# The last group's first six pairs with w_out as seven half products in 128x32 column tiles, its partial sums kept in SBUF for the last two pairs

## The chip, the cores and the metric

One core of one Trainium2 chip. The time is the device time of one execution in microseconds (us); the kernel before took 267.31 us in the median of three runs (266.57 to 267.91). The comparison is between the kernel before and the kernel with the change, both on one core.

## The reference, cut to what matters

A polynomial-sketch attention makes a matrix `x` of 4352 tokens by 128 features (4 heads of 32). That matrix goes through a two-layer block with an ELU between, and this block is where the change is:

```
h = x @ w_in                      # 4352x128 @ 128x2048
g = np.where(h > 0.0, h, np.exp(np.minimum(h, 0.0)) - 1.0)
out = (g @ w_out).astype(np.float32)   # 4352x2048 @ 2048x128
```

All of it is in 32-bit floats.

## The kernel before, in words

The 4352 tokens are cut into NQ = 9 groups: groups 0 to 7 have 512 tokens, the last, group 8, has 256 (`qn[8]` is 2, times 128). The 2048 hidden features are NP = 8 pairs `cp` of two blocks of 128. A *step* is one (group, pair). The list `steps` (lines 901 and 902) fixes their order; groups 2 to 8 go one after another, each through its eight pairs. The order of instructions on every engine is the order of the Python text (`manual_schedule`), and waits between engines are put in by the framework where a tile is read or written.

The main loop (lines 995 to 1033) does this in turn number n:

- `mm1(g, cp)`, line 768: TensorE makes `h`, two banks (c = 0, 1) of 128 features by the group's tokens. It goes through `quarters` (line 223), which splits one product in four matmuls with 32 columns of the stationary operand each, on the four 128x32 column tiles of the array. `h` has four banks, so two steps are in flight.
- `elu`, line 800: ScalarE makes relu(-h) and then exp of its negative (lines 789, 791); VectorE makes `gg` = max(e - 1, h) (line 797). `gg` has three buffers.
- For groups 2 to 7 (`seven(g)`) `sums7` (line 700) makes four sums of quarters of `gg` on GpSimd.
- The product with w_out for the step of two turns ago. For groups 0 and 1 it is `mm2`. For groups 2 to 7 it is `mm2_seven` (line 713), Strassen's scheme in Winograd's form: seven products of half size in place of eight, accumulated over the pairs in seven columns of two PSUM banks `pa` and `pb`. The sums of w_out that it needs are in `SS`, made once by `weights7` (line 692). At a group's end `fin_seven_copy`, `fin_seven_a` and `fin_seven_b` (lines 733 to 766) put the seven sums together on ScalarE and VectorE, transpose them in 32x32 blocks and send them out in 16 DMAs, all issued by SyncE (SP), line 765.
- For group 8 it is `mm2_last` (line 826): `gg` is the stationary operand, w_out the moving one (128 columns), so the output has tokens on partitions and needs no transpose. Per pair it has four products (two blocks c, two token halves i), each four column tiles: 16 matmuls of 128 columns. They accumulate in two PSUM tiles `ol`. `fin_last` (line 836) copies one tile with ScalarE and the other with VectorE and sends each in two DMAs, one issued by SP and one by ScalarE.

A 32-bit matmul stands in the trace as two records, and so does its weight load (LDWEIGHTS, row PEld).

Of the kernel before, what the change touches and what calls it, by code (L numbers as in the profile page):

```python
# [12 lines left out]
F32 = mybir.dt.float32  # L13
ALU = mybir.AluOpType
U32 = mybir.dt.uint32
MUL, ADD, SUB, MAX = ALU.mult, ALU.add, ALU.subtract, ALU.max
# [6 lines left out]
def _ap(ap: bass.AP, free):  # L23
    return dataclasses.replace(ap, ap=[list(ap.ap[0])] + [list(x) for x in free])
# [3 lines left out]
def kernel(  # L28
# [21 lines left out]
    nc = tc.nc  # L50
    B, H, S, D = q.shape
    R = S1.shape[0]
    P = 128
# [3 lines left out]
    NP = NC // 2  # L57
# [7 lines left out]
    work = ctx.enter_context(tc.tile_pool(name="wk", bufs=2))  # L65
    psum = ctx.enter_context(tc.tile_pool(name="psum", bufs=2, space=bass.MemoryType.PSUM))
# [82 lines left out]
    W = const.tile([P, NP, 4 * P], F32, name="W")  # L149
# [73 lines left out]
    def quarters(dst, lhs, rhs, **kw):  # L223
        for c in range(4):
            nc.tensor.matmul(dst[32 * c:32 * c + 32], lhs[:, 32 * c:32 * c + 32], rhs, skip_group_check=True,  # L225
                             tile_position=(0, 32 * c), **kw)
# [226 lines left out]
    NQ = (NH + 7) // 8  # L453
# [6 lines left out]
    def half_tile(g, k):  # L460
        return divmod(8 * g + k, NT)
# [218 lines left out]
    hs, es, gs, ops = {}, {}, {}, {}  # L680
# [5 lines left out]
    def seven(g):  # L686
        return 2 <= g < NQ - 1

    SS = const.tile([P, 4, NP, 64], F32, name="SS")
    ts, acc, sas = {}, {}, {}  # L690
# [6 lines left out]
    def quarter(g, cp, c, y):  # L697
        return gs[g, cp][:, c].rearrange("p (u x s) -> p u x s", u=2, x=2)[:, :, y, :]

    def sums7(g, cp, c):  # L700
        if c == 0:
            ts[g, cp] = work.tile([P, 4, 2, P], F32, name="tt", tag="raw", bufs=6)
        t = ts[g, cp]
        b11, b12 = (quarter(g, cp, 0, y) for y in range(2))
        if c == 0:
            nc.gpsimd.tensor_tensor(t[:, 0], b12, b11, op=SUB)  # L706
            return
        b21, b22 = (quarter(g, cp, 1, y) for y in range(2))
        nc.gpsimd.tensor_tensor(t[:, 2], b22, b12, op=SUB)  # L709
        nc.gpsimd.tensor_tensor(t[:, 1], t[:, 2], b11, op=ADD)  # L710
        nc.gpsimd.tensor_tensor(t[:, 3], b21, t[:, 1], op=SUB)  # L711

    def mm2_seven(g, cp, first, last):
        if first:
            acc[g] = [psum.tile([P, 512], F32, name="pa", tag="o0", bufs=1),
                      psum.tile([P, 512], F32, name="pb", tag="o1", bufs=1)]
        a, b = acc[g]
        t, w = ts.pop((g, cp)), [W[:, cp, 2 * P + 64 * i:2 * P + 64 * i + 64] for i in range(4)]
        b11, b21, b22 = quarter(g, cp, 0, 0), quarter(g, cp, 1, 0), quarter(g, cp, 1, 1)
        p1, p2, p6 = (a, 0, w[0], b11), (a, 1, w[2], b21), (a, 2, SS[:, 1, cp], t[:, 1])  # L720
        p4, p5 = (b, 0, w[3], t[:, 3]), (b, 1, SS[:, 0, cp], t[:, 0])
        p7, p3 = (b, 2, SS[:, 2, cp], t[:, 2]), (b, 3, SS[:, 3, cp], b22)
        todo = [p1, p2, p6, p3, p5, p7, p4] if first or last else [p1, p2, p3, p5, p7, p6, p4]
        for i, (bank, col, lhs, rhs) in enumerate(todo):
            for u in range(2):
                for w in range(2):
                    r = 64 * u + 32 * w
                    nc.tensor.matmul(bank[r:r + 32, P * col:P * col + P], lhs[:, 32 * w:32 * w + 32], rhs[:, u],  # L728
                                     start=(first and i in (0, 3)), stop=last, skip_group_check=True,
                                     tile_position=(0, r))  # L730
        del gs[g, cp]
# [14 lines left out]
    def fin_seven_b(g):  # L746
        b = acc.pop(g)[1]
        uu, cc = sas.pop(g)
        pb = b[:].rearrange("p (k s) -> p k s", s=P)
        nc.vector.tensor_tensor(uu[:, 1:], _ap(uu[:, 0], [[0, 2], [1, P]]), pb[:, 1:3], op=ADD)  # L750
        nc.vector.tensor_tensor(cc[:, 2:], _ap(uu[:, 2], [[0, 2], [1, P]]), pb[:, 0:2], op=ADD)
        nc.vector.tensor_tensor(cc[:, 1], uu[:, 1], pb[:, 3], op=ADD)
        ob = work.tile([P, 2, 4, 2, D], F32, name="ob7", tag="ob", bufs=2)
        nc.vector.transpose(ob[:].rearrange("p h k w d -> p (h k w d)"), cc[:].rearrange("p k s -> p (k s)"))
        rows = out.rearrange("(b w y t) (e l d) -> b w e l y t d", b=B, w=2, t=NT, e=2, l=2)
        for u in range(2):
            k = 0
            while k < 4:
                bt, t = half_tile(g, 4 * u + k)
                m = min(4 - k, NT - t)  # L760
                for lo in range(2):
                    r = slice(64 * u + 32 * lo, 64 * u + 32 * lo + 32)
                    for hi in range(2):
                        for w in range(2):
                            nc.sync.dma_start(rows[bt, w, hi, lo, :, t:t + m, :], ob[r, hi, k:k + m, w, :])
                k += m

    def mm1(g, cp, cs=(0, 1)):
        n = qn[g] * P
        if 0 in cs and (g, cp) not in hs:  # L770
            hs[g, cp] = [psum.tile([P, 512], F32, name="h", tag="h", bufs=4) for c in range(2)]
        for c in cs:
            quarters(hs[g, cp][c][:, :n], W[:, cp, c * P:c * P + P], xg[g][:, :n])
# [8 lines left out]
    def elu_a(g, cp, c, parts=(0, 1)):  # L782

        n = qn[g] * P
        if c == 0 and 0 in parts:
            es[g, cp] = work.tile([P, 2, 512], F32, name="e", tag="e", bufs=2)
        e = es[g, cp][:, c, :n]
        if 0 in parts:
            nc.scalar.activation(e, hs[g, cp][c][:, :n], RELU, scale=-1.0)  # L789
        if 1 in parts:  # L790
            nc.scalar.activation(e, e, EXP, scale=-1.0)  # L791
# [8 lines left out]
    def elu(g, cp, c):  # L800
        elu_a(g, cp, c)
        elu_d(g, cp, c)
# [23 lines left out]
    def mm2_last(cp, first, last):  # L826
        g = NQ - 1
        if first:
            ops[g] = [psum.tile([P, P], F32, name="ol", tag=t, bufs=k) for t, k in (("o0", 1), ("aux", 2))]
        gg = gs.pop((g, cp))  # L830
        for a in range(4):
            c, i = (a % 2, a // 2) if last else divmod(a, 2)
            quarters(ops[g][i][:], gg[:, c, i * P:i * P + P], W[:, cp, (2 + c) * P:(3 + c) * P],
                   start=(first and c == 0), stop=(last and c == 1))

    def fin_last():
        g, n = NQ - 1, qn[NQ - 1]
        o = work.tile([P, 2, P], F32, name="ol", tag="ol", bufs=1)
        rows = out.rearrange("(b y t) f -> b y t f", b=B, t=NT)
        for i, copy in enumerate((nc.scalar.copy, nc.vector.tensor_copy)):  # L840
            copy(o[:, i, :], ops[g][i][:])
            for u, eng in enumerate((nc.sync, nc.scalar)):
                b, t = half_tile(g, u * n + i)
                eng.dma_start(rows[b, :, t, :], o[64 * u:64 * u + 64, i])
# [150 lines left out]
    for n in range(2, N + 2):  # L995
        if n < N:
            g, cp = steps[n]
            mm1(g, cp)
        for f, *a in extra.get(n, ()):
            f(*a)  # L1000
        if n < N:
            elu(g, cp, 0)
            if seven(g):
                sums7(g, cp, 0)
            for f, *a in extra.get((n, 0), ()):
                f(*a)
            before = steps[n - 2]
            ends = n > 3 and seven(before[0]) and before[1] == NP - 1
            if ends:
                elu_a(g, cp, 1, (0,))  # L1010
                mm2_seven(*before, False, True)
                fin_seven_copy(before[0])
                elu_a(g, cp, 1, (1,))
                fin_seven_a(before[0])
                elu_d(g, cp, 1)
            else:
                elu(g, cp, 1)
            if seven(g):
                sums7(g, cp, 1)
            if ends:  # L1020
                fin_seven_b(before[0])
        for f, *a in extra.get((n, 1), ()):
            f(*a)
        g, cp = steps[n - 2]
        if g == NQ - 1:
            mm2_last(cp, cp == 0, cp == NP - 1)
        elif seven(g):
            if cp < NP - 1:
                mm2_seven(g, cp, cp == 0, False)
        elif n > 2:  # L1030
            mm2(g, cp, cp == 0, cp == NP - 1)
            if cp == NP - 1:
                fin1(g)
    fin_last()


# [27 lines left out]
```

## Time and profile before

| what | value |
|---|---|
| median of three runs | 267.31 us |
| the profiled execution's own time | 267.85 us |
| its span in the trace | 266.1 us |
| TensorE busy | 259.1 us (97%) |
| VectorE, ScalarE, GpSimd busy | 187.8, 184.0, 160.6 us |
| granted TensorE clock | full speed in all slices after the first |
| group 8's `mm1`, 128x256 matmuls | 8.4 us busy, x128 records |
| group 8's `mm2_last`, 128x128 matmuls | 8.1 us busy, x256 records |
| output DMAs of one group of 512 (line 765) | 16 issues by SP, 16 KB each for group 7 |
| DMA queue q8, kind "instruction" | 42 packets, 0.69 MB |

"Busy" is the union of the records of an engine; matmuls are pipelined, so a busy TensorE need not be at its peak. "SPq" and "ACTq" are the sequencers of SyncE and ScalarE: their records are issues of DMAs and waits for semaphores. A timeline line gives start, length, engine, line, operation and how many records it merges.

### The profile page before, as it was taken

What the parts mean: (1) busy time and instruction counts of PE and PEld (TensorE: products, weight loads), DVE (VectorE), ACT (ScalarE), POOL (GpSimd) and SP (SyncE); (2) the same over time, 40 slices, a digit from 0 to 9 for tenths busy, and PEclk for the clock granted to TensorE, in tenths of its full rate; (3) what the DMA queues carried; (4) which work ended last, traced back from release to release, by engine and by line L of the source; (5) the groups of instructions that cost most, each with busy time, mean ns of one, the idle gap of its engine ahead of it and who ended that gap; (6) DMA issues with size and microseconds to landing.
All of it is one profiled execution on the core that took longest, in us unless ns stands there. A gap on an engine that the chain in (4) does not pass through costs nothing.

```text
span 266.1 us, 12146 instructions
## 1 busy us (share of the span) xinstructions
PE 259.1 (97%) x5345; PEld 151.6 (57%) x5345; DVE 187.8 (71%) x347; ACT 184.0 (69%) x355; POOL 160.6 (60%) x233
## 2 busy tenths in 40 slices
PE   8999999999999999999999999999999999999993
PEld 7742223343334665667666666665666666657872
DVE  7799999997969796996567676744356446664641
ACT  2479978677567656785587777776777777777781
POOL 4400008204316985798859799898689888998200
PEclk9999999999999999999999999999999999999999
DMA  5999960011002200001100110001001100110011
GB/s 184 320 352 242 288 171 8 2 25 62 2 2 43 42 4 2 2 8 19 27 3 2 28 20 2 2 15 25 11 2 21 25 4 5 18 17 11 7 25 37
DMA packets 26420, 13.89 MB, mean 52 GB/s; under 512 B 19200, under 2 KB 24576, under 8 KB 26368
## 3 DMA queue, kind: packets, MB, share of 16 engines
q1 hardware_dynamic: 25920, 12.79, 19.0%
q8 instruction: 42, 0.69, 1.1%
q10 hardware_dynamic: 448, 0.33, 0.4%
q14 instruction: 10, 0.08, 0.1%
HBM read 10.88 MB, written 2.23 MB: 49 GB/s over the span
## 4 chain that ended last, share of the span: by engine, by line
PE 92%; DVE 4%; POOL 1%; issue 1%; ACT 0%; DVEq 0%
PE h L225 43%; PE pb L728 16%; PE pa L728 12%; PE o L225 11%; PE ol L225 3%; PE kv L390 1%; PE idle L230 1%; PE h L644 1%; PE qps L644 1%; DVE qp L582 1%; POOL kp L286 1%; PE kfps L322 1%; PE qps L538 1%; PE kv L225 1%; PE abp L303 1%
## 5 line engine op out<-in xcount | busy, mean ns | idle before, releaser
L797 DVE SCALAR_TENSOR_TENSOR gg<-e,h 128x512 f32<-128x512 f32 (+1 forms) x144 | 92.2, 653 | 63.3 <-ACT e L791 60.5
L225 PE MATMUL h<-xg,W 128*32 128x512 f32 (+1 forms) x1168 | 130.4, 563 | 0.0
L789 ACT ACTIVATE e<-h 128x512 f32<-128x512 f32 (+1 forms) x144 | 81.4, 566 | 49.6 <-PE h L225 48.1
L791 ACT ACTIVATE e<-e 128x512 f32<-128x512 f32 (+1 forms) x144 | 87.6, 608 | 4.4
L225 PEld LDWEIGHTS h<-xg,W 128*32 128x32 f32 x1168 | 38.4, 110 | 49.0 <-issue 38.9
L706 POOL TENSOR_TENSOR tt<-gg 128x256 f32<-128x256 f32 x48 | 35.4, 737 | 16.0 <-DVE gg L797 15.6
L709 POOL TENSOR_TENSOR tt<-gg 128x256 f32<-128x256 f32 x48 | 35.6, 742 | 13.4 <-DVE gg L797 13.2
L711 POOL TENSOR_TENSOR tt<-gg,tt 128x256 f32<-128x256 f32 x48 | 36.7, 765 | 3.8
L710 POOL TENSOR_TENSOR tt<-tt,gg 128x256 f32<-128x256 f32 x48 | 35.4, 738 | 3.8
L728 PEld LDWEIGHTS pa<-gg,W 128*32 128x32 f32 x768 | 22.8, 110 | 23.4 <-issue 22.4
L225 PE MATMUL o<-gg,W 128*32 128x512 f32 x256 | 30.6, 594 | 0.4 <-DVE W L129 0.4
L728 PE MATMUL pa<-gg,W 128*32 128x128 f32 x768 | 30.4, 273 | 0.0
L728 PE MATMUL pb<-tt,SS 128*32 128x128 f32 x768 | 30.3, 273 | 0.0
L728 PEld LDWEIGHTS pb<-tt,SS 128*32 128x32 f32 x768 | 22.5, 110 | 0.0
L728 PE MATMUL pb<-tt,W 128*32 128x128 f32 x384 | 20.1, 273 | 0.0
L728 PE MATMUL pb<-gg,SS 128*32 128x128 f32 x384 | 19.8, 273 | 0.0
L728 PE MATMUL pa<-tt,SS 128*32 128x128 f32 x384 | 19.8, 273 | 0.0
L126 POOL TENSOR_TENSOR raw<-raw,tiny 128x512 f32<-128x512 f32 x1 | 1.0, 1046 | 29.9 <-DVE raw L121 29.9
L225 PEld LDWEIGHTS o<-gg,W 128*32 128x32 f32 x256 | 7.8, 109 | 16.6 <-issue 14.2
L728 PEld LDWEIGHTS pb<-tt,W 128*32 128x32 f32 x384 | 12.1, 110 | 0.2 <-issue 0.2
L728 PEld LDWEIGHTS pa<-tt,SS 128*32 128x32 f32 x384 | 12.0, 110 | 0.0
L728 PEld LDWEIGHTS pb<-gg,SS 128*32 128x32 f32 x384 | 11.9, 110 | 0.1
(150 smaller groups left out, 245.4 us busy)
## 6 DMA issues: line engine op xcount, KB each, us to landing
raw<-in_moe_w_in_dram SPq DMA_DIRECT2D x8, 256.0 KB, 6.4
raw<-in_moe_w_out_dram SPq DMA_DIRECT2D x8, 256.0 KB, 6.5
hd_k<-in_k_dram SPq DMA_DIRECT2D x3, 544.0 KB, 7.3
hd_q<-in_q_dram SPq DMA_DIRECT2D x3, 544.0 KB, 7.8
v<-in_v_dram SPq DMA_DIRECT2D x4, 288.0 KB, 6.8
out_dram<-ob SPq DMA_DIRECT2D x72, 16.0 KB, 1.5
v<-in_v_dram SPq DMA_DIRECT2D x4, 256.0 KB, 6.6
out_dram<-ob SPq DMA_DIRECT2D x16, 32.0 KB, 1.6
```

The lines of the kernel that those rows point to most:

```text
L225: nc.tensor.matmul(dst[32 * c:32 * c + 32], lhs[:, 32 * c:32 * c + 32], rhs, skip_group_check=True, tile_position=(0, 32 * c), **kw)
L230: nc.tensor.matmul(idle[:, :cols], some[:, :P], some[:, :cols], skip_group_check=True)
L286: eng.tensor_mul(dst, _ap(a_, list(a_.ap[1:]) + [[0, R]]), _ap(b_, [b_.ap[1], [0, R], b_.ap[2]]))
L644: nc.tensor.matmul(ps[w][s * r:s * r + s, 64 * k:64 * (k + m)], lhs, qpT[g, i][rows, o + 2 * k:o + 2 * (k + m), f, :], start=(f == 0 and j ...
L706: nc.gpsimd.tensor_tensor(t[:, 0], b12, b11, op=SUB)
L709: nc.gpsimd.tensor_tensor(t[:, 2], b22, b12, op=SUB)
L710: nc.gpsimd.tensor_tensor(t[:, 1], t[:, 2], b11, op=ADD)
L711: nc.gpsimd.tensor_tensor(t[:, 3], b21, t[:, 1], op=SUB)
L728: nc.tensor.matmul(bank[r:r + 32, P * col:P * col + P], lhs[:, 32 * w:32 * w + 32], rhs[:, u], start=(first and i in (0, 3)), stop=last, s ...
L789: nc.scalar.activation(e, hs[g, cp][c][:, :n], RELU, scale=-1.0)
L791: nc.scalar.activation(e, e, EXP, scale=-1.0)
L797: nc.vector.scalar_tensor_tensor(gs[g, cp][:, c, :n], es[g, cp][:, c, :n], -1.0, hs[g, cp][c][:, :n], op0=ADD, op1=MAX)
```

## The change

For group 8 the pairs 0 to 5 go through seven half products as well, pairs 6 and 7 stay as they were. `b11, b12` and `b21, b22` are the two token halves of blocks c = 0 and c = 1. The sums of `gg` are made by `sums7_last`: two by GpSimd, two by VectorE. The sums of w_out come from `SS`, which is there already. Each of the seven products is four column tiles with 64 columns moving: 28 matmuls per pair. They accumulate over the six pairs in seven columns of 64 of one bank `pl`. After pair 5, `fin_seven_last` puts these into `cl` (two token halves by 128 outputs) with one copy on ScalarE and five additions on VectorE. It is called in the last turn with an `mm1`, after that turn's ELU. Pairs 6 and 7 accumulate in `ol` in PSUM as before, and `fin_last` adds `cl` and `ol`, both halves on VectorE.

```
     def mm2_last(cp, first, last):
...
-            ops[g] = [psum.tile([P, P], F32, name="ol", tag=t, bufs=k) for t, k in (("o0", 1), ("aux", 2))]
+            ops[g] = [psum.tile([P, P], F32, name="ol", tag=t, bufs=k) for t, k in (("o0", 1), ("o1", 1))]
...
+    def sums7_last(cp, c):
+        g = NQ - 1
+        (b11, b12), (b21, b22) = [[gs[g, cp][:, x, P * y:P * y + P] for y in range(2)] for x in range(2)]
+        if c == 0:
+            ts[g, cp] = work.tile([P, 4, P], F32, name="tl", tag="raw", bufs=6)
+        t = ts[g, cp]
+        if c == 0:
+            nc.gpsimd.tensor_tensor(t[:, 0], b12, b11, op=SUB)
+        else:
+            nc.vector.tensor_tensor(t[:, 2], b22, b12, op=SUB)
+            nc.vector.tensor_tensor(t[:, 1], t[:, 2], b11, op=ADD)
+            nc.gpsimd.tensor_tensor(t[:, 3], b21, t[:, 1], op=SUB)
+
+    def mm2_seven_last(cp, first, last):
+        g = NQ - 1
+        if first:
+            acc[g] = psum.tile([P, 512], F32, name="pl", tag="aux")
+        gg, t, w = gs.pop((g, cp)), ts.pop((g, cp)), [W[:, cp, 2 * P + 64 * i:2 * P + 64 * i + 64] for i in range(4)]
+        b11, b21, b22 = gg[:, 0, :P], gg[:, 1, :P], gg[:, 1, P:2 * P]
+        todo = [(0, w[0], b11), (1, w[2], b21), (6, SS[:, 3, cp], b22), (4, SS[:, 0, cp], t[:, 0]),
+                (5, SS[:, 2, cp], t[:, 2]), (2, SS[:, 1, cp], t[:, 1]), (3, w[3], t[:, 3])]
+        for i, (col, rhs, lhs) in enumerate(todo):
+            quarters(acc[g][:, 64 * col:64 * col + 64], lhs, rhs, start=(first and i == 0), stop=last)
+
+    def fin_seven_last():
+        g = NQ - 1
+        pl = acc.pop(g)[:, :448].rearrange("p (k d) -> p k d", d=64)
+        sa = work.tile([P, 2, 64], F32, name="sl", tag="sl", bufs=1)
+        uu = work.tile([P, 3, 64], F32, name="ul", tag="ul", bufs=1)
+        cl = sas[g] = work.tile([P, 2, 2, 64], F32, name="cl", tag="cl", bufs=1)
+        nc.scalar.copy(sa[:], pl[:, 1:3])
+        nc.vector.tensor_tensor(uu[:, 0], sa[:, 1], pl[:, 0], op=ADD)
+        nc.vector.tensor_tensor(cl[:, 0, 0], sa[:, 0], pl[:, 0], op=ADD)
+        nc.vector.tensor_tensor(uu[:, 1:], _ap(uu[:, 0], [[0, 2], [1, 64]]), pl[:, 4:6], op=ADD)
+        nc.vector.tensor_tensor(cl[:, :, 1], _ap(uu[:, 2], [[0, 2], [1, 64]]), pl[:, 3:5], op=ADD)
+        nc.vector.tensor_tensor(cl[:, 1, 0], uu[:, 1], pl[:, 6], op=ADD)
+
     def fin_last():
...
-        for i, copy in enumerate((nc.scalar.copy, nc.vector.tensor_copy)):
-            copy(o[:, i, :], ops[g][i][:])
+        cl = sas.pop(g)
+        for i in range(2):
+            nc.vector.tensor_tensor(o[:, i, :], cl[:, i].rearrange("p h d -> p (h d)"), ops[g][i][:], op=ADD)
...
             elu(g, cp, 0)
             if seven(g):
                 sums7(g, cp, 0)
+            if g == NQ - 1 and cp < NP - 2:
+                sums7_last(cp, 0)
...
             if ends:
                 fin_seven_b(before[0])
+            if g == NQ - 1 and cp < NP - 2:
+                sums7_last(cp, 1)
...
-        if g == NQ - 1:
-            mm2_last(cp, cp == 0, cp == NP - 1)
+        if g == NQ - 1 and cp < NP - 2:
+            mm2_seven_last(cp, cp == 0, cp == NP - 3)
+            if cp == NP - 3:
+                fin_seven_last()
+        elif g == NQ - 1:
+            mm2_last(cp, cp == NP - 2, cp == NP - 1)
```

## The prediction

> **What bounds the kernel now.** I read the page's chain first, then the chain in order of time, then the end of the timeline. On the page TensorE holds nearly all of the chain:
>
> ```profile
> PE 259.1 (97%) x5345; PEld 151.6 (57%) x5345; DVE 187.8 (71%) x347; ACT 184.0 (69%) x355; POOL 160.6 (60%) x233
> ...
> PE 92%; DVE 4%; POOL 1%; issue 1%; ACT 0%; DVEq 0%
> ```
>
> In order of time its last lines (start, length) are:
>
> ```profile
> 256.26 0.86 PE h L225 x16
> 257.13 0.87 PE ol L225 x32
> 258.00 0.86 PE h L225 x16
> 258.86 2.66 PE ol L225 x96
> ```
>
> A step of the last group is 0.86 + 0.87 = 1.73 us, without a gap. But TensorE ends at 261.5 and the span at 266.1. What lies behind shows in the timeline of the other engines:
>
> ```profile
> 251.49 9.97 SPq L765 DMA_DIRECT2D out_dram<-ob  x16
> 261.56 2.36 SPq L844 DMA_DIRECT2D out_dram<-ol  x2
> ```
> ```profile
> 261.11 0.27 ACT L841 COPY ol<-ol 128x128 f32<-128x128 f32 x1 [1.06 <-PE ol L225]
> 261.41 1.77 ACTq L844 DMA_DIRECT2D out_dram<-ol  x2
> ```
> ```profile
> 261.55 0.29 DVE L841 COPY ol<-ol 128x128 f32<-128x128 f32 x1 [1.04 <-PE ol L225]
> ```
>
> The reader is to see that SP issues DMAs without a pause from 251.49 to 263.92. First come the 16 output DMAs of group 7, up to 261.46, then the two of group 8. The first result was there at 261.38 and the second at 261.84, but SP issued the second from 263.29 only, because the issue before it took long:
>
> ```profile
> L844 SPq DMA_DIRECT2D out_dram<-ol x2: 630/1131/1632, 261.6 to 263.3; - x2
> ```
>
> So the end hangs on SP's queue, and TensorE is about level with it. Issues of line 765 take 430 ns, a few far more. The DMA view says which. Two stretches, 255.2 to 258.3 and 258.15 to 261.5:
>
> ```profile
> q8 instruction: 1, 0.02, 2.1%
> out_dram<-ob SPq DMA_DIRECT2D x5, 16.0 KB, 2.7
> ```
> ```profile
> out_dram<-ob SPq DMA_DIRECT2D x7, 16.0 KB, 1.5
> ```
> ```profile
> L765 SPq DMA_DIRECT2D out_dram<-ob x7: 430/431/437, 258.2 to 261.0; - x7
> ```
>
> The second has no instruction packet and every issue is short; the first has one, at 256.73, and the issue begun at 256.59 took 1536 ns. The same holds at 251.93 (issue 1839 ns) and 261.56 (1632 ns). An issue in progress ends some 0.37 us after the packet (251.93 + 1.39, issue over at 253.69). In SP's last 12.4 us three such packets cost 1.41 + 1.11 + 1.00 = 3.52 us above 430 ns (630 for the last).
>
> **What the Trainium skill says.** "Runtime: NRT & Kernel Launch", section Instruction fetch mechanics: instructions come in 16 KiB blocks of 256, each sequencer's fetch driven by its own DMA queue, the cost mostly hidden. The size agrees: 42 packets of 0.69 MB together are 16.4 KB each, and TensorE's 2 x 5345 records are 41.8 blocks. "Mostly hidden" holds for TensorE, not for SP's issues. "TensorEngine Tiling (Array Packing)", section Performance Considerations: a matmul has some 60 cycles of overhead, so short moving operands gain nothing below that. 64 columns is near this edge; the trace has that shape (below) and it is still in proportion. "SBUF — State Buffer", section Who interferes with whom: a VectorE operation with two SBUF inputs contends with a GpSimd operation reading SBUF. The trace agrees: line 563 at 128x128 took 574 ns beside GpSimd, line 565 with one input in PSUM 288.
>
> **The change part by part.** Times from the profiled execution (span 266.06, own time 267.85; the median is 267.31).
>
> *TensorE.* Removed per pair: 32 records of 128 columns, 0.87 us, 27.2 ns each. Added: 56 of 64 columns. The same shape, 128x64 on 128x32 tiles with a new weight load each, ran here:
>
> ```profile
> 10.01 1.21 PE L390 MATMUL kv<-kp,v 128*32 128x64 f32 x72
> ```
>
> One record is 0.22 us long, so 71 starts took 0.99 us: 13.9 ns each. 56 x 13.9 = 0.78 us; gain 0.09 per pair, 0.55 over six. Bounds: 13.6 (half of 27.2; gain 0.65), and, if the 110 ns loads did not hide, 14 turns of the four tiles x 110 = 1.54 us, a loss of 4.0 over six.
>
> *Sums.* Per pair GpSimd gets two 128x128 operations, VectorE two. GpSimd is idle after 247.8; line 252, 128x128, took 402 ns. For VectorE the bounds are 293 (line 571 with GpSimd idle) and 574; I take 293, since GpSimd runs mostly at other times. VectorE then has about 0.35 + 0.42 + 2 x 0.32 = 1.4 us a step, under the new pitch of 0.86 + 0.78 = 1.64; ScalarE's four take about 1.45 from start to start. Behind VectorE's sums in its queue stands the next `gg`, for which the `h` banks wait; two steps of lead leave about 0.85 us. One place has no lead: pair 1, whose sums stand behind group 7's transpose (line 754, to 251.46). The two take until about 252.0, GpSimd's until 252.5, and the seventh product could otherwise start at 252.3 (250.00 + 0.78 + 0.86 + 0.66): a stall of about 0.35 us, 0 if that order is kinder. TensorE is left with about 0.2 us (0 to 0.65).
>
> At 574 ns VectorE needs 1.97 us a step, 0.33 too long; five steps make 1.65, less 0.85 of lead: results 0.8 us later.
>
> *Tail.* `fin_seven_last` stands behind the last ELU on ScalarE and VectorE, whose last `gg` starts 2.26 us after the last `mm1` starts (260.08 - 257.82). Then a copy (0.27) and five additions, in lines 743 to 752 0.2 apart when independent and 0.45 when dependent at double width; at 128x64 and 128x128 I reckon 0.15 and 0.32. The fifth starts about 3.4 after that `mm1`, line 881's two additions at 3.55 and 3.8, done at 4.1; before, the two copies were done at 3.56 and 4.02. With the `mm1` 0.1 earlier, the first result comes 0.3 us later than before (261.7), the second at 261.9, as before. The gain on TensorE ends here.
>
> *SP's queue.* No DMA is added, and group 7's 16 start at the same 251.49. But six pairs have 24 records more in matmuls and as many in loads: 6 x 48 = 288 instructions, 1.1 blocks. And the blocks come sooner: 112 + 32 = 144 instructions per 1.64 us, in place of 96 per 1.73. The packet of 251.93 came some 116 instructions after the first w_out products of the group began (250.00); now that is 250.8. It holds SP from 251.49 until 250.8 + 1.39 + 0.37 = 252.56 in place of 251.81: 0.75. The next come every 256 instructions, some 2.9 us: about 254, 257 and, slower since pairs 6 and 7 are as before, 260 to 261. SP is busy throughout, so each costs the mean of the three, 1.17: 3.52. In all 4.27 for 3.52 before: **+0.75 us**. If the packet comes only after 251.5, the first costs up to 1.41: +1.4. If the fourth does not come, -0.4. Both L884 issues on SP then start after 262.6, when their data (261.7, 261.9) lies ready.
>
> Sum: 266.06 + 0.75 = 266.8 of span, 268.6 for such an execution, and 267.31 + 0.75 = **268.0 us** for the median.
>
> **The rivals.**
> *A: the gain arrives.* If SP is ahead outside the profile, or the fourth packet falls away, the results set the end: between 0.5 us earlier (no stall, short tail) and level. For it: the chain names TensorE. Against: SP's record without a gap. About 267.0.
> *B: slower by over 0.5%* (1.34 us; about what a measurement of this kernel can tell from no change). One mechanism: every one of four packets hits an issue of SP in full. It decides from a mean of (3.52 + 1.34) / 4 = 1.21 us per packet; the three seen have 1.17, the largest 1.41. About 268.8. Against: the first should fall before 251.49.
> *C: the change doesn't do what it says*, 64-column products being no faster than the loads: +4.0, 271.3. Line 390 speaks against it.
> *D: VectorE's sums at 574 ns:* results at 262.7, still no later than SP's 262.6 to 263; about 268.1.
>
> **How the numbers follow.** Forecast 0.55 (267.4 to 268.5), A 0.25, B 0.13, C 0.02, D 0.05. The range leaves out C, part of B and A's far end, with three runs spread by 0.6 either way: 266.6 to 268.9. Faster by over 0.5% (under 265.97) would take all of A and more: 0.03. Slower by over 0.5% (over 268.65): B and C, with little else, 0.14. The rest, 0.83, is within.
>
> **What would show it.** Right: `pl` groups of 0.78 us; one gap in TensorE of some 0.3 us in the second; four instruction packets after 250.5, not three, and SP's last issue ending at about 264.6 in place of 263.92. Wrong: SP idle before L884's issues, or three packets only; then A. `pl` groups over 0.87: C. Line 847 and 848 over 0.5 us: D.

## The result, and the profile after

| | before | after |
|---|---|---|
| median, same chip, 11 runs each | 267.21 us (266.46 to 268.45) | 268.85 us (268.59 to 270.65) |
| ratio after/before, 95% interval | | 1.0072 (1.0053 to 1.0090) |
| profiled execution, its span | 267.85, 266.1 us | 269.15, 267.1 us |
| median span of many runs | 265.1 us (45 runs) | 266.7 us (11 runs) |

Slower by 0.7%, 1.6 us. The last row sets the profiles in place: the one execution of the kernel before that was profiled lies 1 us above that kernel's median span, that of the changed kernel 0.4 us above its own. Where the time went is in the timeline of TensorE. First the head of the page and the chain, of the changed kernel:

```profile
PE 259.2 (97%) x5489; PEld 150.5 (56%) x5489; DVE 192.8 (72%) x365; ACT 183.8 (69%) x355; POOL 165.6 (62%) x245
...
PE 89%; DVE 7%; ACT 2%; issue 1%; POOL 0%; DVEq 0%
```

144 matmul records and 144 load records more, as counted. The busy time of TensorE is all but the same, so the page shows no loss. The timeline of TensorE does (start, length, what, records, and in brackets the idle time before and the releaser that the trace infers). The first five lines are an undisturbed pair:

```profile
249.85 0.41 PE L225 MATMUL pl<-W,gg 128*32 128x64 f32 x16
250.07 0.29 PE L225 MATMUL pl<-SS,gg 128*32 128x64 f32 x8
250.19 0.52 PE L225 MATMUL pl<-SS,tl 128*32 128x64 f32 x24
250.52 0.29 PE L225 MATMUL pl<-W,tl 128*32 128x64 f32 x8
250.63 1.05 PE L225 MATMUL h<-xg,W 128*32 128x256 f32 x16
...
251.83 0.52 PE L225 MATMUL pl<-SS,tl 128*32 128x64 f32 x24
252.41 0.32 PE L225 MATMUL pl<-W,tl 128*32 128x64 f32 x8
...
253.75 0.52 PE L225 MATMUL pl<-SS,tl 128*32 128x64 f32 x24
254.37 0.32 PE L225 MATMUL pl<-W,tl 128*32 128x64 f32 x8
...
257.34 0.29 PE L225 MATMUL pl<-SS,tl 128*32 128x64 f32 x8
258.37 0.43 PE L225 MATMUL pl<-SS,tl 128*32 128x64 f32 x16 [0.73 <-DVE gg L797]
...
260.37 1.06 PE L225 MATMUL ol<-W,gg 128*32 128x128 f32 x32
262.37 1.08 PE L225 MATMUL ol<-W,gg 128*32 128x128 f32 x32 [0.94 <-DVE cl L873]
```

The pair's seven products start at 249.85 and the next `h` at 250.63: 0.78 us. So the products are as fast as the prediction said. But there are four gaps. Read them by starts, since a record's end is modelled: `pl` x24 is followed after 0.33 us in the first pair, after 0.58 in the second (252.41 - 251.83) and after 0.62 in the third; 8 records of `pl` take 0.11 us, but 257.34 to 258.37 is 1.03; 32 records of `ol` take 0.87, but 260.37 to 262.37 is 2.00. The gaps are 0.25, 0.29, 0.92 and 1.13 us, 2.59 together, against 0.55 gained. The kernel before has no such gap:

```profile
250.00 1.06 PE L225 MATMUL ol<-W,gg 128*32 128x128 f32 x32
...
258.68 2.80 PE L225 MATMUL ol<-W,gg 128*32 128x128 f32 x96
```

The 96 records are those of pairs 5, 6 and 7, so pair 7 starts at 258.68 + 2 x 0.87 = 260.42. From the group's first w_out product to that of pair 7 it is 12.52 us (249.85 to 262.37), and was 10.42: TensorE is 2.1 us later.

SP's queue in the changed kernel:

```profile
251.35 11.83 SPq L765 DMA_DIRECT2D out_dram<-ob  x16
263.40 1.19 SPq L884 DMA_DIRECT2D out_dram<-ol  x2
```

And VectorE's last additions:

```profile
263.08 0.72 DVE L881 TENSOR_TENSOR ol<-cl,ol 128x128 f32<-128x128 f32 x2 [0.75 <-PE ol L225]
```

SP is through with group 7 at 263.18, and the first result is there at 263.37: now the result comes last, and SP's first issue of line 884 follows it at once (263.40); the second, at 264.05, stands behind the first, 0.25 us after its data. Instruction packets came at 251.74, 255.51 and 259.43; the next only at 268.21, after the span.

### The profile page after: what moved, and what is told of

The parts are those of the page before. It is cut to its first block, busy times and chain, and to the rows that moved or that the text cites. A ratio compares the mean times of both kernels' runs of the same rounds, so it can differ in the third digit from the quotient of the medians.

```text
span 267.1 us, 12465 instructions
## 1 busy us (share of the span) xinstructions
PE 259.2 (97%) x5489; PEld 150.5 (56%) x5489; DVE 192.8 (72%) x365; ACT 183.8 (69%) x355; POOL 165.6 (62%) x245
## 4 chain that ended last, share of the span: by engine, by line
PE 89%; DVE 7%; ACT 2%; issue 1%; POOL 0%; DVEq 0%
PE h L225 41%; PE pb L728 15%; PE pa L728 12%; PE o L225 11%; PE kv L390 1%; PE idle L230 1%; PE h L644 1%; PE qps L644 1%; DVE gg L797 1%; PE abp L303 1%; ACT e L791 1%; DVE qp L582 1%; ACT e L789 1%; PE kfps L322 1%; PE qps L538 1%
## 5 line engine op out<-in xcount | busy, mean ns | idle before, releaser
L225 PEld LDWEIGHTS h<-xg,W 128*32 128x32 f32 x1168 | 37.4, 110 | 49.3 <-issue 40.1
L728 PE MATMUL pb<-tt,W 128*32 128x128 f32 x384 | 19.5, 273 | 0.0
```

## The experiments

**Three theories.** *F, supply of instructions:* TensorE runs dry. Count its instructions from the first `pl` product (every record of a matmul has one of a load, so x56 is 112). A pair with its `h` is 112 + 32 = 144. The third gap of the list above lies in pair 4 after 32 records: 4 x 144 + 64 = 640. The second lies in pair 2 after 48 records: 2 x 144 + 96 = 384. The fourth lies behind pair 5 (832, no `h` follows) and pair 6's 64: 896. They are 256 apart, one block as in the prediction. Each ends 1.35 to 1.49 us after an instruction packet is through (251.74 + 1.20, 255.51 + 1.51, 259.43 + 1.45; gaps end at 254.37, 258.37, 262.37). *S, sums* (W in the expectations)*:* TensorE waits for the new sums and for `cl`, which is what the view of waits says for 257 to 263 us of the changed kernel:

```profile
PE ol L225 <- DVE cl L873: 0.9, 1, 0.9
...
PE pl L225 <- DVE gg L797: 0.7, 1, 0.7
```

But pair 7's product `ol` has no use for `cl`, and VectorE's sums of pair 4, which come next in that product, were done by 256.11, over 2 us before TensorE went on at 258.37. By contrast, GpSimd ends the last sum of pair 1 at 252.36, and TensorE goes on at once, at 252.41. The two sums (the first line is GpSimd's, the second VectorE's):

```profile
251.90 0.46 POOL L849 TENSOR_TENSOR tl<-gg,tl 128x128 f32<-128x128 f32 x1 [2.69 <-DVE tl L848]
...
255.82 0.29 DVE L848 TENSOR_TENSOR tl<-tl,gg 128x128 f32<-128x128 f32 x1
```

*Q*, the prediction's own, is the third: SP's queue sets the end.

**The sums left out.** The four sums are not made, and the products read quarters of `gg` instead:

```
-            nc.gpsimd.tensor_tensor(t[:, 0], b12, b11, op=SUB)
...
-            nc.gpsimd.tensor_tensor(t[:, 3], b21, t[:, 1], op=SUB)
+        ts[g, cp] = [b12, b22, b12, b21]
```

> The changed kernel with the sums of gg left out: the seven products take quarters of gg in their place, so TensorE's instructions are the same, and GpSimd and VectorE have no sums to make. Theory F (instruction supply): TensorE runs dry at block ends of 256 instructions, because a block takes some 4.0 us from one fetch to the next and six seven-product steps ask for one every 2.9 us. Then the gaps of about 0.3, 0.9 and 1.2 us stay at the same instructions, only the first gap of 0.25 us (second pair, real wait for GpSimd) goes, and the time is 268.3 to 269.0 us. Theory W (waits for the sums, as the trace's view of waits names them): the gaps go, and the time falls to 267.3 or less.

Measured: 268.36 us, ratio to before 1.0047 (1.0031 to 1.0063). TensorE's timeline in this run:

```profile
256.87 0.41 PE L225 MATMUL pl<-SS,gg 128*32 128x64 f32 x16
257.46 0.43 PE L225 MATMUL pl<-SS,gg 128*32 128x64 f32 x16 [0.18 <-issue]
...
259.46 1.06 PE L225 MATMUL ol<-W,gg 128*32 128x128 f32 x32
260.91 1.08 PE L225 MATMUL ol<-W,gg 128*32 128x128 f32 x32 [0.39 <-DVE cl L862]
```

The gaps stand at the same instructions, 384, 640 and 896, and the one at 640, for which the changed kernel's trace names `gg`, is now put down to nothing ("issue"). By starts they are 0.17, 0.36 and 0.58 us, so smaller: TensorE went on 3.45 us apart here (257.46, 260.91) and 4.00 there. This execution is a fast one, 267.54 us, where the median is 268.36. The gap in pair 1 is gone: that one was a real wait, for GpSimd (line 849). S is out as the main cause: without any sums 1.3 us of the 1.6 stay in the medians, and the rest is about pair 1's 0.25.

**More instructions, no sums.** The kernel before, with each 128-column product of pairs 0 to 5 cut into two of 64:

```
+            for y in ((0, 1) if cp < NP - 2 else (slice(0, P),)):
+                y = y if isinstance(y, slice) else slice(64 * y, 64 * y + 64)
+                quarters(ops[g][i][:, y], ..., W[:, cp, (2 + c) * P:(3 + c) * P][:, y], ...
```

> The kernel before, with each 128-column product of pairs 0 to 5 of the last group cut in two of 64 columns: no sums, no new engine work, the same columns on TensorE, but 32 matmuls a pair in place of 16, so 160 instructions (loads and matmuls, two records each) per 1.73 us. Theory F: gaps at block ends, about one block per 4.0 us, TensorE ends 2 to 3 us later, time 269 to 270 us. Theory W: no gap, 267.2 us. Theory Q (the queue of SyncE sets the end and only fetches that hold its issues count): 267.5 to 268.5 us, without gaps on TensorE.

Measured: 268.6 us, ratio 1.0053 (1.0033 to 1.0073), a little less than expected. TensorE:

```profile
255.86 1.05 PE L225 MATMUL h<-xg,W 128*32 128x256 f32 x16
257.36 1.10 PE L225 MATMUL ol<-W,gg 128*32 128x64 f32 x64 [0.45 <-issue]
...
259.14 0.85 PE L225 MATMUL ol<-W,gg 128*32 128x64 f32 x48
261.09 2.18 PE L225 MATMUL ol<-W,gg 128*32 128x64 f32 x80 [1.09 <-issue]
```

The same arithmetic and the same operands, with nothing new to wait for, lose 0.5% (the changed kernel 0.7%). From 257.36 to 261.09 TensorE went through 64 + 16 + 48 = 128 records, 256 instructions, in 3.73 us.

**SP relieved.** Eight of the 16 output DMAs of group 7 are left out (that half of its output is missing), in the changed kernel and in the one before:

```
-                        for w in range(2):
+                        for w in range(1 if g == NQ - 2 else 2):
```

> The changed kernel with 8 of the 16 output DMAs of group 7 left out (half of that group's result is not written), so that SyncE's queue is free long before the end. Theory F: TensorE and the last additions set the end now (results at 263.4 and 263.8 us in the trace), the gaps stay, and the time falls by 0.0 to 0.4 us only. Theory Q: the end follows the queue, 1 us or more earlier.

> The kernel before with the same 8 DMAs left out. If SyncE's queue sets the end of the kernel before, as the prediction has it, the second output DMA of the last group starts at about 262.0 in place of 263.29 unless an instruction packet holds it; time 0.5 to 1.2 us lower, 266.0 to 266.7 us. If TensorE sets it, no change: 267.2 us.

Measured: changed 268.46 us, 1.0049 (1.0031 to 1.0067); before 266.92 us, 0.9994 (0.9976 to 1.0012). The first agrees with F: the gaps stay, and its median lies 0.4 us under the 268.85 of the changed kernel. The second is a miss of mine: of the two cases I had taken Q's, 0.5 to 1.2 us less, and no gain can be told; the interval leaves room for 0.6 us. So SP's queue does not explain the loss, and in the typical execution of the kernel before it sets the end by little or not at all.

**The blocks shifted.** 20 small matmuls (80 instructions) ahead of the group, in the changed kernel:

```
+    for i in range(20):
+        nc.tensor.matmul(idle[32 * (i % 4):32 * (i % 4) + 32, :32], some[:, :32], some[:, :32], ...
```

> The changed kernel with 20 small matmuls more (32x32 columns, into the scratch tile) at the start, where TensorE waits anyway: 80 instructions more ahead of the last group. Theory F (a block of 256 instructions must have been fetched): the gaps move 80 instructions forward in the stream and stay 256 apart: from the fourth part of the third seven-product group to its start, from the middle of the fifth group to the mm1 ahead of it, from between the last two 128-column products to the end of the sixth seven-product group. Time as the changed kernel, 268.2 to 269.2 us. Theory W (waits for VectorE and GpSimd): the gaps stay at the same matmuls.

Measured: 269.68 us, 1.0103 (1.0057 to 1.0149); slower than expected (268.2 to 269.2). The group began late (first `pl` at 251.67, not 249.85); why is open. TensorE:

```profile
257.65 0.61 PE L225 MATMUL h<-xg,W 128*32 128x256 f32 x8
258.68 0.64 PE L225 MATMUL h<-xg,W 128*32 128x256 f32 x8 [0.41 <-DVE gg L800]
...
261.12 0.52 PE L225 MATMUL pl<-SS,tl 128*32 128x64 f32 x24
262.13 0.32 PE L225 MATMUL pl<-W,tl 128*32 128x64 f32 x8 [0.50 <-issue]
262.27 1.93 PE L225 MATMUL ol<-W,gg 128*32 128x128 f32 x64
...
263.61 0.21 DVE L876 TENSOR_TENSOR cl<-ul,pl 128x64 f32<-128x64 f32 x1
```

Two of the three gaps moved by the 80 instructions put in front: into the middle of an `h`, after 8 of its 16 records (4 x 112 + 3 x 32 + 16 = 560 = 640 - 80), and into pair 5 (816 = 896 - 80). At 304 = 384 - 80 there is none: TensorE came there at 255.34, 1.80 us after the packet was through (252.20 + 1.34), and the gaps here end 1.34 and 1.36 us after theirs. The middle of an `h` has no new data to wait for; it needs a free bank, and the ELU of pair 4 had left that at 257.16 (line 800, 256.42 + 0.74), 1.5 us before. Pair 7 now follows pair 6 without a gap, at 263.14 (262.27 + 0.87), before `cl` is done (263.61 + 0.21), so it does not wait for `cl` either. With this F stands as shown.

**How much is too much.** The changed kernel with half products for pairs 0 to 2 only; and the kernel before with all the sums made and read by nobody:

```
-            if g == NQ - 1 and cp < NP - 2:
+            if g == NQ - 1 and cp < 3:
...
-            mm2_seven_last(cp, cp == 0, cp == NP - 3)
+            mm2_seven_last(cp, cp == 0, cp == 2)
```

> The changed kernel with seven half products for pairs 0 to 2 only, pairs 3 to 7 as before. 144 instructions more than before instead of 288. Theory F: the first block end after the group's start falls where its fetch is just done (some 254.4 us), the next 256 instructions take 4.2 us of TensorE's time, no gap over 0.2 us; TensorE keeps 0.1 to 0.3 us of gain, time 266.6 to 267.3 us, so about 1.5 us under the change with six pairs, though half of the pairs are changed. If each changed pair costs its share (sums, waits, VectorE's additions at the end): half of the loss stays, 267.9 us.

> The kernel before with the sums of gg for pairs 0 to 5 of the last group made on GpSimd and VectorE as in the change, but read by nobody; TensorE's stream is that of before. Theory F: no loss beyond 0.3 us, 267.0 to 267.4 us, no gap on TensorE. Theory W (the sums hold up gg and with it TensorE): gaps before the last products, 267.8 us or more.

Measured: three pairs 267.38 us, 1.0012 (0.9998 to 1.0026); sums alone 266.86 us, 0.9993 (0.9973 to 1.0013). So the sums cost nothing that can be told (267.0 to 267.4 was expected). Three pairs in a row lose 0.25 us at one block end and 0.25 in pair 1, more than the 0.27 they gain; the time is just above the range expected, which had no gap over 0.2.

**The supply by itself.** The kernel before, and after its last copies 400 matmuls of 64 columns, with no data to wait for:

```
+    sc = psum.tile([P, 512], F32, name="sc", tag="h", bufs=4)
+    for i in range(100):
+        quarters(sc[:, :64], some[:, :P], some[:, :64])
```

> The kernel before, and after its last copies 400 more matmuls of 64 columns on 128x32 tiles (1600 instructions with their loads) into a spare bank; their result is used by nobody. TensorE waits for nothing in them. If the supply of instructions is the limit: bursts of at most 128 matmul records (256 instructions, 1.8 us at 13.9 ns a record) with a gap after each, the bursts 3.4 to 4.0 us apart, about 22 us for the stream, and instruction packets at the same distance. If TensorE's supply keeps up: 800 records at 13.9 ns, 11 us without a gap.

Its timeline of TensorE:

```profile
261.21 1.88 PE L225 MATMUL sc<-some 128*32 128x64 f32 x112
263.85 1.99 PE L225 MATMUL sc<-some 128*32 128x64 f32 x128 [0.76 <-issue]
267.85 1.99 PE L225 MATMUL sc<-some 128*32 128x64 f32 x128 [2.01 <-issue]
271.31 1.99 PE L225 MATMUL sc<-some 128*32 128x64 f32 x128 [1.46 <-issue]
275.31 2.66 PE L225 MATMUL sc<-some 128*32 128x64 f32 x128 [2.01 <-issue]
```

Bursts of exactly 128 records, 256 instructions, most done in about 2 us and then up to 2 us of nothing; they start 4.00, 3.46 and 4.00 us apart. (The first 112 records belong to a block begun earlier.) The last burst shown took 2.66 us because the granted TensorE clock is 0.50 from 276.4 us on, after 1.00 before; the next burst still starts 3.73 us later, at 279.04. Other DMA traffic isn't the cause: from 266 us on the DMA queues moved five instruction packets and nothing else. The packets show how a turn is made up: each starts 1.03 to 1.15 us after a burst begins (264.98, 269.00, 272.35, 276.34), takes 1.03 to 1.51, and the next burst begins 1.28 to 1.59 us after it is through. What makes a turn 3.46 us in one case and 4.00 in another is open.

**Spread out.** Half products for pairs 0, 2 and 4, plain pairs between, so that the instructions come more evenly:

```
-            if g == NQ - 1 and cp < NP - 2:
+            if g == NQ - 1 and cp in (0, 2, 4):
...
```

> The kernel with the change, but only pairs 0, 2 and 4 of the last group go through the seven half products; pairs 1, 3, 5, 6 and 7 stay plain. Nothing is left out. The half products are the same three as in the run with pairs 0 to 2, spread out, so that no stretch of 256 instructions has more than two of them. If the supply of instructions is what stops TensorE: block ends at instruction 384 and 640 after the first group of half products come at about 255.0 and 259 us, and the gaps there are 0 to 0.2 us, not 0.3 and 0.7; the wait of pair 1 for GpSimd is gone as well, since pair 1 needs no sums; 266.6 to 267.2 us, level with the kernel before or up to 0.2% below. If the end hung on SyncE's queue instead, the extra packet would still come: 267.5 to 268.

Measured: 267.25 us, 1.0001 (0.9987 to 1.0014). TensorE has no gap and gains what three pairs should (3 x 0.09 us): its last result is there 11.57 us after the group's first w_out product (250.06 to 261.63), and 11.84 in the run with sums alone (249.76 to 261.60). Yet the time is the same, just above the range expected. SP in this run:

```profile
251.55 11.00 SPq L765 DMA_DIRECT2D out_dram<-ob  x16
262.65 1.22 SPq L884 DMA_DIRECT2D out_dram<-ol  x2
```

In the run with sums alone, where two packets hit SP and not three:

```profile
251.25 9.24 SPq L765 DMA_DIRECT2D out_dram<-ob  x16
261.17 1.19 SPq L857 DMA_DIRECT2D out_dram<-ol  x2
```

So here, with TensorE out of the way, SP's queue is last, as Q has it. To test that, eight of the 16 DMAs were left out of this kernel too; and, as a version that leaves nothing out, four of them went to GpSimd, two behind its sums of pair 2 and two behind those of pair 4:

```
+                            if g == NQ - 2 and w and hi:
+                                held.append((dst, src))
...
+                for _ in range(2 if cp else 0):
+                    nc.gpsimd.dma_start(*held.pop(0))
```

> The kernel with half products for pairs 0, 2 and 4 only, and eight of the 16 output DMAs of group 7 left out (that half of its output is missing). TensorE has no gap in the former and its results come 0.27 us sooner than in the kernel before, yet the time is not lower; in its profile SyncE gets to the last output DMAs at 262.6 only, 1 us after the data. If SyncE's queue is what takes the gain there: 0.25 to 0.6 us below the run with all 16, 266.6 to 267.0 us, and both DMAs of the last results start within 0.1 us of their data. If the gain is lost elsewhere: 267.1 to 267.4 us, as with all 16.

> The kernel with half products for pairs 0, 2 and 4 only, with four of the 16 output DMAs of group 7 moved from SyncE to GpSimd: two behind its sums of pair 2, two behind those of pair 4, where it idles. Nothing is left out. SyncE's run of issues gets 4 x 430 ns = 1.7 us shorter and so ends ahead of the first result, and the gain of TensorE (0.27 us) can reach the end: 266.6 to 267.0 us, ratio 0.996 to 0.9995. What it costs on GpSimd no run shows yet: if an issue there takes over 1 us, the sums of pair 4 come late and TensorE waits, or the transfers land last: 267.2 us and more.

Measured: half left out 266.63 us, 0.9963 (0.9946 to 0.9980), so SP's queue did hold this kernel back: with all 16 it was 1.0001 (0.9987 to 1.0014). The kernel before with the same eight left out was 266.92 us, 0.9994; the 0.29 us between the two fits the 0.27 that TensorE gained. Four on GpSimd 267.06 us against 267.40 before, 0.9980 (0.9966 to 0.9995). SP and GpSimd in the latter:

```profile
251.56 7.65 SPq L769 DMA_DIRECT2D out_dram<-ob  x12
261.23 1.19 SPq L888 DMA_DIRECT2D out_dram<-ol  x2
```
```profile
253.34 1.28 POOL L1072 DMA_DIRECT2D out_dram<-ob  x2
...
256.41 1.09 POOL L1072 DMA_DIRECT2D out_dram<-ob  x2
```

SP is free at 259.2 and issues as soon as the result is there. This version is faster than the kernel before by 0.2%, and than the changed kernel by more. That the gain is that of the three pairs is not shown: the kernel before was not run with four DMAs on GpSimd, and its interval with eight left out (0.9976 to 1.0012) takes in 0.2%.

**A side track that failed.** To shorten SP's tail, the kernel before with its last output as two DMAs of 128 partitions in place of four of 64:

```
-            for u, eng in enumerate((nc.sync, nc.scalar)):
...
+            dst = rows[b, :, t:t + n + 1, :].rearrange("y t f -> t y f")[0:n + 1:n]
+            (nc.scalar, nc.sync)[i].dma_start(dst, o[:, i])
```

> The kernel before with the last group's output sent in two DMAs of 128 partitions, the first issued by ScalarE and the second by SyncE, in place of four. If the issue of the second pair behind the first counts at the end (0.5 to 0.6 us an issue), the end comes 0.3 to 0.6 us earlier: 266.5 to 266.8 us. If a DMA of 64 KB lands later by as much, no change.

Measured: 269.44 us, 1.0093 (1.0059 to 1.0127). The issues were as short as those of half the size (655 and 622 ns), but the data moved slowly. The row of DMA activity in tenths, 40 slices from 263 to 267 us of this run:

```profile
DMA  0111111111111111111111111111111100000000
```

In the run with sums alone, 260 to 266 us, the same bytes go in short bursts (the digits from slice 15 on):

```profile
DMA  4203301400000001636053620000000000000000
```

The last byte is out at 266.19 in the run with two DMAs and at 263.59 in the one with four. "DMA: Bandwidth & Descriptors", section Why a DMA increments its semaphore by 16 and not by 1, says that the number of DMA engines that a transfer uses is the largest number up to 16 that divides the slowest dimension (other than 1) of both sides; here the slowest dimension of the destination is 2. The low activity agrees; no run varied that dimension.

## Why the prediction was wrong

It forecast 268.0 us and no measurable change; it was 268.85 and slower by 0.7%. That 268.85 still lies inside its range (266.6 to 268.9) is luck: the loss came by another way than the one it reckoned. By its own steps:

- *`pl` groups of 0.78 us; C excluded:* right (249.85 to 250.63).
- *One stall of about 0.35 us in pair 1, for GpSimd's last sum:* right in place and cause, 0.25 us; it is gone where the sums are left out.
- *VectorE's sums hidden (against D):* right; made without use they cost nothing that can be told (0.9993, 0.9973 to 1.0013).
- *288 instructions more, and blocks needed "every 256 instructions, some 2.9 us":* right as a demand, and **here the prediction failed**. It held these blocks against SP's issues alone and let "'mostly hidden' holds for TensorE" stand. "Runtime: NRT & Kernel Launch", section Instruction fetch mechanics, does say mostly hidden; at 256 instructions per 4.6 us, the kernel before (96 per 1.73), the trace agrees, and at the change's demand it does not. A block was to be had every 3.45 to 4.00 us only, so a demand for one every 2.9 starves TensorE. A warning was there, a packet of 1.0 to 1.4 us in the profile of before and a demand that rose by 60%; but the two waits around a packet, which make 3.45 to 4.00 us of it, only the runs showed. Three of the four gaps, 2.3 us of 2.6, are this term, which stood in the sum at nothing.
- *SP's queue sets the end, four packets in place of three, +0.75:* wrong. With TensorE starved there were three before the last results, not four: 3.8 and 3.9 us apart, not 2.9. The first, forecast for 250.8, came at 251.74, as late after the group's first product as before (1.89 and 1.93 us). They cost SP more each (1616, 2146 and 1905 ns of issue, 4.38 us above 430 ns; 4.27 were forecast for four), but the result at 263.37 was later than SP at 263.18.
- *The profiled execution as the base:* a weak step. Its span, 266.1, was 1 us over the median, 265.1, and its end at SP was not the typical one: relieving SP there gains nothing that can be told (0.9994, 0.9976 to 1.0012). With fewer packets in SP's last issues, results and SP were about level, so a later TensorE showed for the most part: 2.1 us on TensorE, 1.6 on the median span. That the third packet makes the difference between those executions was only argued; it fits that in two runs with TensorE's stream and the last DMAs of before (sums alone, half the outputs) that packet came after the last result (267.13, 265.52) and the spans were 264.8 and 264.9.
- *Rival B* named the right side and about the right time (268.8) by the wrong mechanism. Slower had been given 0.14.
- *One line misread, without consequence:* the 574 ns of line 563 are a mean of three: 287 with GpSimd idle, 762 and 673 beside it. The new sums of line 847 took 250 to 411 ns once the group's products ran.

Open: the changed kernel spends 2.1 us outside its span, the one before 1.8 (medians). This goes with some of the runs with gaps (2.0 with the sums left out, 2.3 with half the outputs) but not with all (1.8 with the products cut in two); its cause was not found.

## What to carry to other kernels

When an edit swaps few long matmuls for many short ones, divide instructions (matmuls and loads) by the time they are to take: here, where it ran dry, TensorE got 256 per 3.5 to 4.0 us and no more, whatever the arithmetic saved. A gap whose named releaser was done long before, and which lies a multiple of 256 instructions from the next such gap, points to supply, not data; the test is to shift the stream by some instructions and see whether it moves, as it did here. Spread short matmuls between long ones, and check what is next in line at the end: the saving of three pairs spread out came to nothing (1.0001) until SP's queue was shortened as well.

## What the runs showed that was not expected

- The supply limit itself: with the array free and no data to wait for, 128 records of a 64-column matmul run in about 2 us at full clock, then TensorE stands still until 3.46 to 4.00 us have gone by.
- From one gap's end to the next, where both lie one block apart, six traces show three distances and no other: 3.45, 3.73 and 4.00 us (14 cases). Why is not known.
- A new block is usable only 1.25 to 1.60 us after its packet is through: so it is at all 21 block ends with a gap, in seven traces. The 11 other block ends in these, from the group's first w_out product on, are reached 1.8 us or more after their packet, and none has a gap.
- The trace named three different releasers for the gap at the same instruction: `gg` in the changed kernel, line 848 with half the outputs left out, "issue" with the sums left out.
- GpSimd issued a 16 KB output DMA in 548 to 730 ns, landing after 1.7 to 2.0 us (four of them), and TensorE had no gap: cheap cover for a crowded SP here.
